# Column sums for the modulation gradients regrouped into runs of 16 and 8 over four strips and two banks, and one w1-gradient piece moved ahead of the last sums

## The chip, the cores and the metric

The kernel runs on one core of a Trainium2 chip. The metric is the device time of one execution in microseconds (us), the median of several runs. Its engines are TensorE (PE, with its weight loads listed apart as PEld), VectorE (DVE), ScalarE (ACT), GpSimdE (POOL) and SyncE (SP). SyncE only issues DMAs here, GpSimdE mostly does.

## The reference

It is the forward and backward pass of one block with adaptive layer norm, in bf16, on 2048 tokens of width 1024 with an MLP of width 3584:

```python
mod = silu(c) @ w_mod                     # six rows of 1024: sa, ca, ga, sb, cb, gb
h = layernorm(x) * (1 + ca) + sa
x = x + ga * irfft2(rfft2(h) * (w_r + 1j * w_i))
h = layernorm(x) * (1 + cb) + sb
out = x + gb * (gelu(layernorm(h) @ w1 + b1) @ w2 + b2)
```

The kernel returns `out` and the gradients by x, w_r, w_i, w1, b1, w2, b2, c and w_mod for a given `grad_out`. The gradient by each of the six modulation rows is a sum over all 2048 tokens, that is, a column sum of a 2048 × 1024 product. These column sums are what the change regroups. From the rows (`d_gmod` in memory) the gradients by w_mod and c follow.

## The kernel before

The work is laid out by the Tile framework. The program calls the operations in some order, a scheduler places them on the engines, and `tc.issue_after` and `behind(ins, later)` tell it that one instruction is to stand after another. Tokens are held as 4 blocks (`b` = 0 to 3, `NB` = 4) of 4 × 128 tokens; `i` is a group of 128 tokens in a block, `h` a half of the 1024 columns (`KH` = 512). The forward pass comes first. Then, in the stretch that matters here:

1. **Backward passes**, `pg_pass(b, h, ...)`: the gradient of a block by the MLP's input, 7 groups `g` × 4 `i` × 4 `k` matmuls `pg<-w1T,gzr` (L1230) into four PSUM banks, for h = 0, then h = 1. "Pass 1, 2, 3" below is b = 1, 2, 3. While PE is in pass b + 1, VectorE and ScalarE work on block b: layer-norm backward (`ln_bwd`, L1370 on VectorE, L1373 on ScalarE, an add at L195) into `gn3` (two buffers in turn, `gn3a`, `gn3b`), the product `pru` = `gn3` · `n2u`, the second layer norm, the residual, the product `au` = gradient · `au` (`au` is loaded from `d_A` at L1521 and multiplied in place), the product with the ga row into `pru`, and the fold of the result for the spectral backward (`fold_quarter`).
2. **Column sums of three rows** for each block: of `gn3`, of `pru`, of `au`. A sum is taken by matmuls against a block of ones, 128 × 32 (`strip_sum`, L217). Their output is only 32 partitions high, a strip; a PSUM bank has four strips (j = 0 to 3). `sums3` (L1398) takes `gn3` into strips 0, 1 of `acc3a` and `pru` into strips 2, 3, one strip for each half h. `sums3_ga` (L1407) takes `au` into all four strips of `acc3b` (`halves_sum`: even and odd `i` apart, added at the end by `store_halves`). The lists `sums_in` hold the matmuls of `sums3` of block b; the next pass puts them behind given matmuls with `behind`: 4 + 4 of `gn3` and 8 of `pru`. The `au` sums come at the end of a pass.
3. **Spectral backward** (`spectral_core`), beside it the products for w2's gradient (`gw2acc`, L1416) and then pieces of w1's gradient (`gw1acc`, L1779; a piece is 16 matmuls and one copy by ScalarE, L1783, and a store by GpSimdE, L1784). `mid_bwd` (L1832) finishes the three rows. `consume_bwd(i, ...)` (L1589) takes the result for block i: layer-norm backward of the first norm, the residual from `d_gx`, the store of x's gradient (two indirect stores, L167), and the column sums `accCA`. `fill(n)` puts n pieces of w1's gradient into PE's stream at that place.
4. **The tail**: the last w1 products by `quad_sums` (sums and differences of operands, seven products for eight; `gqx`, `gqy`, `gqw`, L1695), whose results ScalarE copies (`snap`, L1677) and VectorE combines, and the rest of w_mod's gradient (`otl`, L1299 on ScalarE, stored at L1304 by GpSimdE).

Of the kernel before, what the change touches and what calls it, by code (L numbers as in the profile page):

```python
# [10 lines left out]
FP32 = mybir.dt.float32  # L11
# [8 lines left out]
D = 1024  # L20
# [15 lines left out]
def kernel(  # L36
# [1184 lines left out]
    last_pg = [None]  # L1221
    sums_in = [[], [], []]

    def pg_pass(b, h, pool, before=lambda: ExitStack()):
        pgs = [pool(k)("pg") for k in range(4)]
        for g in range(7):
            for i in range(4):
                for k in range(4):
                    with before():
                        last_pg[0] = nc.tensor.matmul(pgs[i][:], lhsT=gzs[b, g][:, k, i * P:(i + 1) * P],  # L1230
                                                      rhs=w1Ts[g][:, k, h * KH:(h + 1) * KH],
                                                      start=(g == 0 and k == 0), stop=(g == 6 and k == 3))
                    last_pe[0] = last_pg[0]
                g0 = 3 if b == NB - 1 else 2
                if b > 0 and h == 0 and (g, i) in ((g0, 0), (g0 + 1, 2), (g0 + 2, 2)):
                    for ins in sums_in[g - g0]:
                        behind(ins, last_pg[0])
                    sums_in[g - g0].clear()
            for k in range(4 if b < 2 and h == 1 else 0):
# [157 lines left out]

    def sums3(b, g4, p4):  # L1398
        for k, src4 in enumerate((g4, p4)):
            for i in range(4):  # L1400
                for h in range(2):
                    ins = strip_sum(acc3[0], 2 * k + h, src4[:, i, h * KH:(h + 1) * KH], b == 0 and i == 0, b == 3 and i == 3)
                    if b < 3:
                        sums_in[2 * k or i // 2].append(ins)

    def sums3_ga(b, p4):
        halves_sum(acc3[1], p4, b == 0, b == 3)  # L1407

# [48 lines left out]
    for b in range(NB):  # L1457
# [9 lines left out]
        if b > 0:  # L1467
# [10 lines left out]
            for h in range(2):  # L1478
                for _ in pg_pass(b, h, lambda k: ps_f if (8 * (b - 1) + 4 * h + k) % 6 < 4 else ps_s):
                    pass  # L1480
            with tc.issue_after(last_pg[0].ins):
                sums3_ga(b - 1, au)
                if b == NB - 1:
                    gb1_rows()
# [17 lines left out]
        if b < NB - 1:  # L1502
            sums3(b, gn3, pru)
        else:
            g2, ftmp = gn3s[0], gzr[0].rearrange("p a b (c d) -> p (a b c d)", c=1).rearrange("p (q d) -> p q d", d=D)
# [83 lines left out]
    def consume_bwd(i, o4, tmp, tmp2, n1, eb):  # L1589
# [20 lines left out]
        if i < 3:  # L1610
            x1_in = nc.sync.dma_start(out=n1, in_=chunk_rows(d_gx1, i))
        tt(o4, o4, n1 if i < 3 else eb, ALU.add)
        store_tok(out_1, o4, i)
        if i == 1:
            with tc.issue_after(x1_in.ins):
                next(chain)
        fill((4, 1, 2, 2)[i])
        if i == 3:
            for ins in ln_in[-4:]:
                behind(ins, w1g["ev"])  # L1620
        halves_sum(accCA[0], tmp, i == 0, i == 3)
        fill((1, 2, 1, 2)[i])
        if i == 3:
            rows = small.tile([P, D], BF16, tag="gmrow", bufs=1)
            store_halves(accCA[0], rows[0:64, 0:KH], tmp, 1)

# [17 lines left out]
    def quad_sums():  # L1644
# [4 lines left out]
        S3 = reg.tile([P, 8, KH], BF16, name="S3", tag="sma")[:]  # L1649
        tt(T1[:], B12[:], B11[:], ALU.subtract)  # L1650
        tt(T2[:], B22[:], T1[:], ALU.subtract)
# [146 lines left out]
    for cl in (CE, SE):  # L1798
        sm_in = nc.sync.dma_start(out=smA2[:, cl // 2], in_=d_SF[:, cl])
    sums3(3, gn3s[1], pru)  # L1800
    nc.sync.dma_start(out=em2, in_=d_E[:, 0])
# [30 lines left out]
    def mid_bwd():  # L1832
        sums3_ga(3, au)
        rows = small.tile([P, D], BF16, tag="gmrow", bufs=1)
        nc.vector.tensor_copy(out=rows[:, 0:KH], in_=acc3[0][:])
        store_strips(rows[:, 0:KH], 0, 3)
        store_strips(rows[:, 0:KH], 2, 4)
        ins = store_halves(acc3[1], rows[0:64, KH:D], au, 2)
        for step in step_in[3:8]:
            behind(step, ins)  # L1840
# [78 lines left out]
```

## Time and profile before

| | |
|---|---|
| median of 3 runs | 1372.04 us (1367.43 to 1376.55) |
| profiled execution, its own time | 1369.55 us |
| its span | 1367.8 us |
| granted TensorE clock | 0.998 |
| TensorE busy | 1336.9 us, 98% |
| VectorE busy | 1079.9 us, 79% |
| ScalarE busy | 785.1 us, 57% |
| GpSimdE busy | 388.9 us, 28% |

The span goes from the first to the last instruction; some 1.8 us lie around it. All times inside the kernel are counted from the span's start. A timeline row gives the start, the time from the first start to the last end of a group of like instructions, engine, line, operation, output<-inputs, tile, shape and count; in brackets the idle time of the engine before it and what ended that.

### The profile page before, as it was taken

What the parts mean: (1) busy time and instruction counts of PE and PEld (TensorE: products, weight loads), DVE (VectorE), ACT (ScalarE), POOL (GpSimd) and SP (SyncE); (2) the same over time, 40 slices, a digit from 0 to 9 for tenths busy, and PEclk for the clock granted to TensorE, in tenths of its full rate; (3) what the DMA queues carried; (4) which work ended last, traced back from release to release, by engine and by line L of the source; (5) the groups of instructions that cost most, each with busy time, mean ns of one, the idle gap of its engine ahead of it and who ended that gap; (6) DMA issues with size and microseconds to landing.
All of it is one profiled execution on the core that took longest, in us unless ns stands there. A gap on an engine that the chain in (4) does not pass through costs nothing. (4 is left out here: it accounts for less than half of the span.)

```text
span 1367.8 us, 18497 instructions
## 1 busy us (share of the span) xinstructions
PE 1336.9 (98%) x6771; PEld 651.4 (48%) x6899; DVE 1079.9 (79%) x1475; ACT 785.1 (57%) x1112; POOL 388.9 (28%) x436
## 2 busy tenths in 40 slices
PE   6999999999999999999999999999999999999998
PEld 3445566444444444444444444444654555454443
DVE  5997879999988888887611578889888588976996
ACT  4964657667877756665413583446633464544454
POOL 6273542412112122112211011112344330331163
PEclk9999999999999999999999999999999999999999
DMA  9975594899787887697999689998679978899977
GB/s 326 312 209 138 151 267 154 238 280 321 258 256 256 205 265 236 209 280 243 279 290 214 200 206 307 271 285 246 201 220 261 236 158 243 217 235 231 223 259 269
DMA packets 356402, 330.08 MB, mean 241 GB/s; under 512 B 203866, under 2 KB 298736, under 8 KB 356182
## 3 DMA queue, kind: packets, MB, share of 16 engines
q1 hardware_dynamic: 314310, 201.02, 58.1%
q0 software_dynamic: 35232, 120.00, 26.2%
q10 hardware_dynamic: 6768, 7.87, 1.7%
q8 instruction: 54, 0.88, 0.3%
q14 instruction: 38, 0.31, 0.1%
HBM read 165.73 MB, written 114.87 MB: 205 GB/s over the span
## 5 line engine op out<-in xcount | busy, mean ns | idle before, releaser
L1230 PE MATMUL pg<-w1T,gzr 128*128 128x512 bf16 x877 | 194.6, 380 | 1.1 <-issue 0.2
L548 PE MATMUL pp<-gBoT,wt 128*128 128x512 bf16 x810 | 182.8, 379 | 3.6 <-ACT pho L540 1.9
L1076 PEld LDWEIGHTS <-w 128*128 128x128 bf16 x896 | 87.2, 98 | 107.3 <-issue 2.9
L1230 PEld LDWEIGHTS <-gzr 128*128 128x128 bf16 x896 | 86.6, 98 | 108.4 <-issue 5.8
L548 PEld LDWEIGHTS <-wt 128*128 128x128 bf16 x832 | 81.0, 98 | 97.3 <-issue 4.8
L1779 PE MATMUL gw1acc<-gzh,n3n 128*128 128x512 bf16 x500 | 111.1, 380 | 0.6
L1076 PE MATMUL pz<-n3Ta,w 128*128 128x512 bf16 x440 | 98.4, 380 | 1.9 <-ACT gt L1079 1.4
L1076 PE MATMUL pz<-n3Tb,w 128*128 128x512 bf16 x438 | 98.3, 380 | 0.5
L1779 PEld LDWEIGHTS <-n3n 128*128 128x128 bf16 x640 | 62.4, 98 | 75.0 <-issue 1.3
L195 DVE TENSOR_TENSOR ct<-ct 128x2048 bf16<-128x2048 bf16 (+1 forms) x84 | 91.5, 1119 | 4.3 <-ACT n L514 2.0
L1079 ACT ACTIVATE gt<-pz,b_col 128x512 bf16<-128x512 f32 x112 | 72.8, 682 | 37.2 <-PE pz L1076 30.9
L1130 PEld LDWEIGHTS <-hhA 128*128 128x128 bf16 x608 | 58.9, 98 | 73.1 <-issue 2.8
L1087 ACT ACTIVATE gt<-gt 128x2048 bf16<-128x2048 bf16 x28 | 53.5, 1911 | 58.3 <-DVE gt L195 58.3
L1416 PE MATMUL gw2acc<-gB,hhsA 128*128 128x512 bf16 x373 | 84.1, 380 | 0.6
L195 DVE TENSOR_TENSOR gt<-gt,gt 128x2048 bf16<-128x2048 bf16 x56 | 68.4, 1223 | 17.7 <-ACT gt L1089 16.8
L1424 ACT CAST gwo<-gw2acc 128x512 bf16<-128x512 f32 x40 | 23.6, 589 | 87.5 <-PE gw2acc L1416 84.6
L1416 PEld LDWEIGHTS <-hhsA 128*128 128x128 bf16 x384 | 37.6, 98 | 43.4
L1783 ACT CAST gwo<-gw1acc 128x512 bf16<-128x512 f32 x40 | 23.1, 579 | 59.0 <-PE gw1acc L1779 53.8
L1083 ACT ACTIVATE gt<-gt 128x2048 bf16<-128x2048 bf16 x28 | 53.4, 1908 | 3.1 <-DVE hhC L195 2.4
L540 ACT CAST pho<-pp 128x512 bf16<-128x512 f32 x68 | 38.6, 583 | 27.3 <-PE pp L548 24.1
L1089 ACT ACTIVATE gt<-gt 128x2048 bf16<-128x2048 bf16 x28 | 53.4, 1906 | 0.3
L1416 PE MATMUL gw2acc<-gB,otl 128*128 128x512 bf16 x220 | 49.4, 380 | 0.2
(415 smaller groups left out, 2699.7 us busy)
## 6 DMA issues: line engine op xcount, KB each, us to landing
gzr<-d_gz SPq DMA_DIRECT2D x28, 512.0 KB, 4.5
d_ph<-pho POOLq DMA_DIRECT2D x21, 512.0 KB, 6.4
wblk<-in_w_mod_dram SPq DMA_DIRECT2D x10, 1024.0 KB, 7.2
out_dram<-otl POOLq DMA_DIRECT2D x40, 256.0 KB, 4.4
d_hh<-hhA POOLq DMA_DIRECT2D x19, 512.0 KB, 5.9
wrw<-in_w_mod_dram SPq DMA_DIRECT2D x32, 256.0 KB, 5.3
w<-in_B_w_dram SPq DMA_DIRECT2D x7, 1024.0 KB, 11.5
hhC<-d_ph SPq DMA_DIRECT2D x14, 512.0 KB, 3.7
```

The costliest lines, as they stand in the source:

```text
L195: return nc.vector.tensor_tensor(out=out, in0=a, in1=b, op=op)
L540: copy(out=ov, in_=pv)
L548: last_pe[0] = nc.tensor.matmul(pp[:], lhsT=wt[:, fc % 4, cch, :], rhs=gBoT[j][:, cch, :], start=(cch == 0), stop=(cch == NDC - 1))
L1076: last_pe[0] = nc.tensor.matmul(pz[:], lhsT=w1s[g][:, cch, k * P:(k + 1) * P], rhs=n3T[:, cch, :], start=(cch == 0), stop=(cch == NDC - 1))
L1079: z_in = nc.scalar.activation(out=zb[:, k, :], in_=pz[:], func=ACT.Identity, bias=b1_col[:, fc:fc + 1], scale=1.0)
L1083: nc.scalar.activation(out=av, in_=zb, func=ACT.Square)
L1087: nc.scalar.activation(out=sg, in_=bv, func=ACT.Sigmoid, scale=2.0 * GK)
L1089: nc.scalar.activation(out=bv, in_=bv, func=ACT.Sigmoid, scale=-2.0 * GK)
L1130: last_pe[0] = nc.tensor.matmul(pbs[i][:], lhsT=hh[:, k, i * P:(i + 1) * P], rhs=wp[:, k, :], start=False, stop=(g == 6 and k == 3))
L1230: last_pg[0] = nc.tensor.matmul(pgs[i][:], lhsT=gzs[b, g][:, k, i * P:(i + 1) * P], rhs=w1Ts[g][:, k, h * KH:(h + 1) * KH], start=(g == 0 ...
L1416: nc.tensor.matmul(acc[:], lhsT=hh_of(fc)[:, t, :], rhs=gBs[t // 4][:, t % 4, h * KH:(h + 1) * KH], start=(t == 0), stop=(t == NT - 1))
L1779: nc.tensor.matmul(acc[:], lhsT=n3ns[t // 4][:, t % 4, cch * P:(cch + 1) * P], rhs=gz2[t // 8][:, t % 8, :], start=(t == 0), stop=(t == NT ...
```

## The change

It has three parts, and the scheduler rearranges some neighbours with them.

- **Sums.** In each pass there are two places instead of three: `at` is ((3,1), (4,2)) for passes 1 and 2, ((3,2), (5,2)) for pass 3. At the first stand the 8 sums of `gn3`, and in passes 2 and 3 woven with them, two by two, the 8 sums of `au` of the block before, which until now had a run of their own at the end of the pass. `gn3` goes to strips 0, 1 of `acc3a`, `au` to strips 2, 3 of `acc3b`. At the second stand the 8 sums of `pru`, of even `i` into strips 2, 3 of `acc3a`, of odd `i` into strips 0, 1 of `acc3b`. Block 3's sums are written in woven order. The `au` sums at the end of pass 3 stay.
- **Rows.** `mid_bwd` adds the two parts of the `pru` row from two banks and stores the four halves of two rows at the end.
- **w1 piece.** The last sums `accCA` come one piece (16 matmuls) later: `fill` counts 3 and 1 around them instead of 2 and 2. `issue_after` keeps the residual add `w1g["x1"]` ahead of two operations on VectorE and ScalarE.

```diff
-    sums_in = [[], [], []]
+    sums_in = [[], []]
...
-                g0 = 3 if b == NB - 1 else 2
-                if b > 0 and h == 0 and (g, i) in ((g0, 0), (g0 + 1, 2), (g0 + 2, 2)):
-                    for ins in sums_in[g - g0]:
+                at = ((3, 2), (5, 2)) if b == NB - 1 else ((3, 1), (4, 2))
+                if b > 0 and h == 0 and (g, i) in at:
+                    for ins in sums_in[at.index((g, i))]:
                         behind(ins, last_pg[0])
...
-    def sums3(b, g4, p4):
-        for k, src4 in enumerate((g4, p4)):
-            for i in range(4):
-                for h in range(2):
-                    ins = strip_sum(acc3[0], 2 * k + h, src4[:, i, h * KH:(h + 1) * KH], b == 0 and i == 0, b == 3 and i == 3)
-                    if b < 3:
-                        sums_in[2 * k or i // 2].append(ins)
-
-    def sums3_ga(b, p4):
-        halves_sum(acc3[1], p4, b == 0, b == 3)
+    def col_sum(acc, j, src4, i, h, first, last):
+        return strip_sum(acc, j + h, src4[:, i, h * KH:(h + 1) * KH], first, last)
+
+    def sums3(b, g4, p4, a4):
+        for i in range(4):
+            for h in range(2):
+                sums_in[0].append(col_sum(acc3[0], 0, g4, i, h, b == 0 and i == 0, b == 3 and i == 3))
+            for h in range(2 if 0 < b < 3 else 0):
+                sums_in[0].append(sum_ga(b - 1, i, h, a4))
+            for h in range(2 if b == 3 else 0):
+                col_sum(acc3[0], 2, p4, i, h, False, i == 3)
+        for i in range(4 if b < 3 else 0):
+            for h in range(2):
+                sums_in[1].append(col_sum(acc3[i % 2], 2 - 2 * (i % 2), p4, i, h, b == 0 and i < 2, b == 2 and i == 3))
+        if b == 3:
+            sums_in[0].clear()
+
+    def sum_ga(b, i, h, a4):
+        return col_sum(acc3[1], 2, a4, i, h, b == 0 and i == 0, b == 3 and i == 3)
+
+    def sums3_ga(b, a4):
+        for i in range(4):
+            for h in range(2):
+                sum_ga(b, i, h, a4)
...
-            with tc.issue_after(last_pg[0].ins):
-                sums3_ga(b - 1, au)
-                if b == NB - 1:
+            if b == NB - 1:
+                with tc.issue_after(last_pg[0].ins):
+                    sums3_ga(b - 1, au)
                     gb1_rows()
...
-        tt(o4, o4, n1 if i < 3 else eb, ALU.add)
+        w1g["x1"] = tt(o4, o4, n1 if i < 3 else eb, ALU.add)
...
-        fill((4, 1, 2, 2)[i])
+        fill((4, 1, 2, 3)[i])
...
-        fill((1, 2, 1, 2)[i])
+        fill((1, 2, 1, 1)[i])
         if i == 3:
             rows = small.tile([P, D], BF16, tag="gmrow", bufs=1)
-            store_halves(accCA[0], rows[0:64, 0:KH], tmp, 1)
+            with tc.issue_after(w1g["x1"].ins):
+                store_halves(accCA[0], rows[0:64, 0:KH], tmp, 1)
...
-        tt(T1[:], B12[:], B11[:], ALU.subtract)
+        with tc.issue_after(w1g["x1"].ins):
+            tt(T1[:], B12[:], B11[:], ALU.subtract)
...
-        nc.vector.tensor_copy(out=rows[:, 0:KH], in_=acc3[0][:])
+        odd = au[64:128, 0, :].bitcast(FP32)
+        nc.scalar.copy(out=odd, in_=acc3[1][0:64, :])
+        nc.scalar.copy(out=rows[64:128, KH:D], in_=acc3[1][64:128, :])
+        nc.vector.tensor_copy(out=rows[0:64, 0:KH], in_=acc3[0][0:64, :])
         store_strips(rows[:, 0:KH], 0, 3)
+        ins = tt(rows[64:128, 0:KH], acc3[0][64:128, :], odd, ALU.add)
         store_strips(rows[:, 0:KH], 2, 4)
-        ins = store_halves(acc3[1], rows[0:64, KH:D], au, 2)
+        store_strips(rows[:, KH:D], 2, 2)
```

On PE, in pass 2, before: the end of one full matmul group, the four sums of `gn3b` behind group (2,0), and the next group (LDWEIGHTS is the load of a matmul's weights; `ones_bf` are the ones, `gzr` the pass's operand).

```order
L1230 MATMUL pg<-w1T_5957,gzr_5941 128x512
L218 LDWEIGHTS ones_bf
L218 MATMUL acc3a<-gn3b,ones_bf 32x512
L218 LDWEIGHTS ones_bf
L218 MATMUL acc3a<-gn3b,ones_bf 32x512
L218 LDWEIGHTS ones_bf
L218 MATMUL acc3a<-gn3b,ones_bf 32x512
L218 LDWEIGHTS ones_bf
L218 MATMUL acc3a<-gn3b,ones_bf 32x512
L1230 LDWEIGHTS gzr_5941
```

And the start of the first run of pass 2 now, behind group (3,1); it goes on like this to 16.

```order
L1230 MATMUL pg<-w1T_5963,gzr_5941 128x512
L218 LDWEIGHTS ones_bf
L218 MATMUL acc3a<-gn3b,ones_bf 32x512
L218 LDWEIGHTS ones_bf
L218 MATMUL acc3a<-gn3b,ones_bf 32x512
L218 LDWEIGHTS ones_bf
L218 MATMUL acc3b<-au,ones_bf 32x512
L218 LDWEIGHTS ones_bf
L218 MATMUL acc3b<-au,ones_bf 32x512
```

The sums of `gn3b` stand later, all eight together, and between two of them stand two of `au`, on other strips and in the other bank.

On SyncE, whose queue goes in order, the loads around block 1 and pass 3, before (`hb` are transposes of the MLP's activations, `gzr` the operand of the passes, `n3u`, `n2u`, `got` rows of the next block):

```order
L1206 DMA gzr2_5943<-d_gz_104 128x4x512
L1521 DMA au_6287<-d_A_98 128x4x1024
L1453 DMA_TRANSPOSE hb_6760<-d_hh_103 128x16x128
L1453 DMA_TRANSPOSE hb_6763<-d_hh_103 128x16x128
L1206 DMA gzr2_5943<-d_gz_104 128x4x512
L1461 DMA n3u_6280<-d_n3_99 128x4x1024
L1463 DMA n2u_6281<-d_x1_97 128x4x1024
L1206 DMA gzr3_5944<-d_gz_104 128x4x512 x2
```

And now:

```order
L1206 DMA gzr2_5943<-d_gz_104 128x4x512
L1467 DMA_TRANSPOSE hb_6760<-d_hh_103 128x16x128
L1467 DMA_TRANSPOSE hb_6763<-d_hh_103 128x16x128
L1206 DMA gzr2_5943<-d_gz_104 128x4x512
L1475 DMA n3u_6280<-d_n3_99 128x4x1024
L1535 DMA au_6287<-d_A_98 128x4x1024
L1477 DMA n2u_6281<-d_x1_97 128x4x1024
L1206 DMA gzr3_5944<-d_gz_104 128x4x512 x2
```

The load of `au` has moved behind two transposes and two loads, since its buffer is read by the sums until later.

On GpSimdE in the tail, before: the stores of w1 pieces, the last two indirect stores of x's gradient, and the stores of w_mod rows.

```order
L1784 DMA out_dram<-gwo_9683 128x512 x11
L167 DMA out_dram<-ct,xu 2048x1024 x2
L1784 DMA out_dram<-gwo_9683 128x512 x2
L1304 DMA out_dram<-otl 128x1024
L1784 DMA out_dram<-gwo_9683 128x512
```

And now:

```order
L1800 DMA out_dram<-gwo_9684 128x512 x12
L167 DMA out_dram<-ct,xu 2048x1024 x2
L1800 DMA out_dram<-gwo_9684 128x512
L1304 DMA out_dram<-otl 128x1024
L1800 DMA out_dram<-gwo_9684 128x512
```

One store of a w1 piece has come ahead of the indirect stores.

More of the change, by code (lines that the diff above doesn't have):

```diff
@@ L1233, in pg_pass @@
                     last_pe[0] = last_pg[0]
[L1234 to L1236 removed]
+                at = ((3, 2), (5, 2)) if b == NB - 1 else ((3, 1), (4, 2))
+                if b > 0 and h == 0 and (g, i) in at:
+                    for ins in sums_in[at.index((g, i))]:
                         behind(ins, last_pg[0])
[L1238 removed]
+                    sums_in[at.index((g, i))].clear()
             for k in range(4 if b < 2 and h == 1 else 0):
@@ L1502 @@
         if b < NB - 1:
-            sums3(b, gn3, pru)
+            sums3(b, gn3, pru, au)
         else:
@@ L1799 @@
         sm_in = nc.sync.dma_start(out=smA2[:, cl // 2], in_=d_SF[:, cl])
-    sums3(3, gn3s[1], pru)
+    sums3(3, gn3s[1], pru, au)
     nc.sync.dma_start(out=em2, in_=d_E[:, 0])
```

## The prediction

> **What bounds the kernel now.** I read the page's first part, then the list of TensorE's waits, then the timelines of the two places that the diff touches. The first part says which engine to follow:
>
> ```profile
> span 1367.8 us, 18497 instructions
> PE 1336.9 (98%) x6771; PEld 651.4 (48%) x6899; DVE 1079.9 (79%) x1475; ACT 785.1 (57%) x1112; POOL 388.9 (28%) x436
> ```
>
> TensorE (PE) is busy in 1336.9 of 1367.8 us. Only what takes time from its stream, or lets it wait, can move the end. The list of PE's waits (engine, line, what it waited for; us in total, times, longest) has these at or behind the places of the change:
>
> ```profile
> PE accCA L218 <- DVE ct L195: 1.3, 1, 1.3
> ...
> PE gqy L1695 <- ACT snap L1677: 0.9, 1, 0.9
> ...
> PE gw2acc L1416 <- issue: 0.3, 2, 0.2
> ```
>
> The first stands ahead of the last column sums, which the moved w1 piece concerns. The second comes 40 us later, in the tail. The third is the largest of PE's waits between 880 and 1275 us, so a lead that PE wins in the backward passes should last until 1275.
>
> A "busy" PE is not at full pace in the column sums. This is PE's timeline (start, us from first start to last end, line, tile, count) of pass 1, of an `au` run with the start of pass 3, and of block 3's run of 16:
>
> ```profile
> 774.49 5.35 PE L1230 MATMUL pg<-w1T,gzr 128*128 128x512 bf16 x23
> 779.77 0.61 PE L218 MATMUL acc3a<-gn3a,ones_bf 128*32 128x512 bf16 x4
> 780.32 3.63 PE L1230 MATMUL pg<-w1T,gzr 128*128 128x512 bf16 x16
> 783.87 1.04 PE L218 MATMUL acc3a<-pru,ones_bf 128*32 128x512 bf16 x8
> 784.85 1.47 PE L1230 MATMUL pg<-w1T,gzr 128*128 128x512 bf16 x6
> ...
> 868.26 0.61 PE L218 MATMUL acc3b<-au,ones_bf 128*32 128x512 bf16 x8
> 868.80 11.40 PE L1230 MATMUL pg<-w1T,gzr 128*128 128x512 bf16 x51
> 880.13 0.61 PE L218 MATMUL acc3a<-gn3a,ones_bf 128*32 128x512 bf16 x4
> 880.67 5.35 PE L1230 MATMUL pg<-w1T,gzr 128*128 128x512 bf16 x23
> ...
> 939.22 1.89 PE L1416 MATMUL gw2acc<-gB,hht 128*128 128x512 bf16 x8
> 941.04 0.39 PE L218 MATMUL acc3a<-gn3b,ones_bf 128*32 128x512 bf16 x2
> 941.07 0.39 PE L218 MATMUL acc3a<-pru,ones_bf 128*32 128x512 bf16 x2
> ...
> 941.73 0.38 PE L218 MATMUL acc3a<-pru,ones_bf 128*32 128x512 bf16 x2
> 942.04 1.69 PE L1416 MATMUL gw2acc<-gB,hht 128*128 128x512 bf16 x6
> ```
>
> The reader is to see what a switch between full matmuls and strip sums costs. By the code 52 full matmuls lie between 868.80 and 880.13 and 24 between 774.49 and 779.77 (a record is missing in each row). With pitch p and entry e (last full matmul to first sum), 51p + e = 11.33 and 23p + e = 5.28, so p = 0.216 us and e = 0.31 us. From the first sum to the next full matmul a run takes the difference of two starts. What a run adds to the stream is e, plus that difference, less the p that the step would take anyway:
> - 4 matmuls on two strips: 780.32 − 779.77 = 0.55, adds 0.64
> - 8 on two strips: 0.98, adds 1.07
> - 8 on four strips (`au`): 0.54, adds 0.64
> - 16 on four strips: 1.00, adds 1.09
>
> Each round of one matmul for every strip takes about p, whether two strips take part or four. A run also pays about 0.2 us for being a run at all. Fewer runs and fuller rounds are the whole mechanism.
>
> **The sums, step by step.** Pass 1 loses 4 + 4 + 8 (two strips), 0.64 + 0.64 + 1.07 = 2.35, and gets one 8 on two strips and one 8 on four, 1.07 + 0.64 = 1.71: **−0.64**. Passes 2 and 3 lose the same 2.35 and get a 16 and an 8 on four strips, 1.09 + 0.64 = 1.73: **−0.62 each**. The two `au` runs at the ends of passes 1 and 2 disappear: **−0.64 each**. Block 3's 16 were already executed two strips and two strips in turn, so their new program order is worth nothing. Together −3.16 us.
>
> One price isn't in the trace: a run whose four strips lie in two banks (`acc3a` and `acc3b`). At best it is the run of 16 above. At worst the banks exclude each other and the rounds go at the pace of two strips: a 16 adds 1.09 + 4 × 0.216 = 1.95, an 8 adds 1.07; pass 1 then saves 2.35 − 2.14 = 0.21, passes 2 and 3 lose 0.67 each, the `au` runs still save 1.28, and of 3.16 there remain 0.15. I take the first, since the row nearest in every other respect (16 matmuls, four strips, two sources) shows it.
>
> From 941.07 to 941.73 three rounds of the run of 16 took 0.66 us, 0.22 each. The Trainium skill speaks against such a pace in "TensorE: Matmul & The Clock Gate", section "Part 3: Packing small matmuls — row/col tiling": it lists a measured speedup of 2.38× with three column tiles, 0.79 for each tile. An estimate from that page: four tiles would give 3.2×, a round 0.27 us, and with ten more rounds on four strips than before (14 less the `au` runs' 4) the sums would save 0.5 us less, 2.6 instead of 3.16. The trace disagrees with its 0.22.
>
> **Earlier sums meet later data.** A run may start when its source is there. VectorE (DVE) and the SyncE queue (SPq), around pass 3; the last two rows are DMA groups of the page (KB each, median us to landing):
>
> ```profile
> 830.55 0.44 SPq L1521 DMA_DIRECT2D au<-d_A  x1
> ...
> 843.20 0.46 SPq L1461 DMA_DIRECT2D n3u<-d_n  x1
> 843.71 0.50 SPq L1463 DMA_DIRECT2D n2u<-d_x  x1
> ...
> 848.59 2.29 DVE L195 TENSOR_TENSOR au<-gn3b,au 128x4096 bf16<-128x4096 bf16 x1
> ...
> 855.90 2.36 DVE L195 TENSOR_TENSOR gn3b<-pru 128x2048 bf16<-128x2048 bf16 x2 [2.83 <-DMA d_gx<-gn3b]
> ...
> 878.96 0.69 DVE L195 TENSOR_TENSOR gn3a<-gn3a,got 128x1024 bf16<-128x1024 bf16 x1
> ...
> 880.41 0.69 DVE L195 TENSOR_TENSOR gn3a<-gn3a,got 128x1024 bf16<-128x1024 bf16 x1 [0.77 <-ACT got L1373]
> ...
> wblk<-in_w_mod_dram SPq DMA_DIRECT2D x10, 1024.0 KB, 7.2
> ...
> w<-in_B_w_dram SPq DMA_DIRECT2D x7, 1024.0 KB, 11.5
> ```
>
> In pass 3 the run of 16 stands behind group (3,2), eight full matmuls behind the old place (3,0). In old time that is 880.67 + 8 × 0.216 = 882.40 for the next start. Off come the run at (3,0), 0.64, and the lead from before, 0.64 + 0.64 + 0.62 + 0.64 = 2.54: 879.22. The first sum would start 0.09 later (e less p), and the fourth round, which takes `gn3a`'s last quarter, at 879.31 + 3 × 0.22 = 879.97. That quarter is ready at 880.41 + 0.69 = 881.10, and this chain is DVE's and ScalarE's (ACT), not PE's. So PE waits about **+1.1 us** with the whole pass behind it. The third quarter (879.65) is just in time.
>
> The second bound on that wait is the `au` load. It was issued at 830.55, before the `hb` transposes; now it stands between the loads of `n3u` and `n2u`, since its buffer is free only after the sums in pass 2. If it is issued near 843.7 and lands as the faster of the two groups of 1024 KB does (7.2), it is there at 850.9, 2.3 us after DVE wanted it at 848.59. Behind that multiply DVE has 2.83 us idle at 855.90, which hides the 2.3. Earlier transposes (1024 KB less ahead of them) make it less. I take 0; the slower group (11.5) would make it 855.2 − 848.59 − 2.83, +3.8, the far end.
>
> **The moved piece, and the end.** PE (with VectorE, ScalarE, GpSimdE, which is POOL) around the last sums and the tail:
>
> ```profile
> 1273.75 3.83 PE L1779 MATMUL gw1acc<-gzh,n3n 128*128 128x512 bf16 x17
> ...
> 1276.56 2.29 DVE L195 TENSOR_TENSOR ct<-ct,xt 128x4096 bf16<-128x4096 bf16 x1
> ...
> 1278.90 0.61 PE L218 MATMUL accCA<-ct,ones_bf 128*32 128x512 bf16 x8 [1.32 <-DVE ct L195]
> ...
> 1299.03 2.29 DVE L195 TENSOR_TENSOR ct<-ct,eb 128x4096 bf16<-128x4096 bf16 x1
> ...
> 1301.61 3.41 POOL L167 DMA_INDIRECT out_dram<-ct,xu  x1 [10.58 <-DVE ct L195]
> ...
> 1309.00 1.31 POOL L1784 DMA_DIRECT2D out_dram<-gwo  x2
> 1310.30 0.54 POOL L1304 DMA_DIRECT2D out_dram<-otl  x1
> ...
> 1312.96 1.15 ACT L1299 ACTIVATE otl<-gr,u_rt 128x1024 bf16<-128x1024 bf16 x1 [4.66 <-DMA out_dram<-otl]
> ...
> 1318.31 0.56 ACT L1677 COPY snap<-gqy 128x512 f32<-128x512 f32 x1
> ...
> 1318.92 1.89 PE L1695 MATMUL gqy<-gzh,ct 128*128 128x512 bf16 x8 [0.88 <-ACT snap L1677]
> ```
>
> Sixteen more full matmuls (16 × 0.216 = 3.46 us) go ahead of the sums and cover the 1.32 us there: −1.32 at that place. But the wait at 1318.92 doesn't hang on PE. The chain is the DVE product (1276.56), the rest of that chain on DVE up to 1299.03, two indirect stores on POOL, the queue of POOL stores, ACT's wait for `otl` to leave, `snap`. A PE that comes 1.32 earlier waits 1.32 longer: +1.32. Of the order on POOL one L1784 store less stands between the indirect stores and the first L1304 (0.65 of the 1.31), so `snap` comes some 0.65 earlier: **−0.65**, the net of the move.
>
> The lead from the passes comes through if the chain shifts with PE. It does where the stage's transposes wait for PE to free their buffers. This row of SyncE's waits, from 1180 to 1290 us, says so:
>
> ```profile
> SPq L1634 <- PE gw1acc L1779: 56.9, 7, 16.1
> ```
>
> What is reordered on DVE, ACT and SyncE between the passes and the spectral stage I cost at nothing: an ACT copy more for the third row (0.56 by the copy at 1318.31), and two more row stores on SyncE ahead of the `hhsA` transpose:
>
> ```profile
> 980.92 0.53 SPq L229 DMA_DIRECT2D d_gmod<-rows  x2
> ```
>
> They lie beside PE's spectral matmuls, where no wait of PE is listed. With that cover gone they would cost 0.56 and 0.53.
>
> **Sum.** −3.16 + 1.1 − 0.65 = −2.7 us on the profiled execution's 1369.55 us. That execution lies 2.5 under the median of the runs (1372.04; they spread over 9 us), and I apply the same difference to the median: **1369.3 us**. Within 1% (13.7 us) is about what a measurement of this kernel can tell from no change.
>
> **Rivals.**
> - *Everything counts* (0.10): `gn3a` is ready in time because DVE's chain comes earlier too, and `snap` follows the product. −3.16 − 1.32 = −4.5: 1367.5. Against it: DVE at 855.90 waited for a store, not for PE.
> - *The tail keeps its own time* (0.20): between 1190 and 1280 the DMA, not PE, sets the product's time, so `snap` stays and every lead ends in the wait before it. Only the 0.65 is left: 1371.4. The row of 56.9 us speaks against it, the 1.32 of waiting for DVE for it.
> - *Two banks exclude each other* (0.07): 0.15 from the sums, no wait in pass 3, 0.65 at the end: 1371.2.
> - *Slower* (0.13): the `au` load. It sits in SyncE's queue ahead of `n2u`, and behind it on DVE stand the multiply, the product with the ga row and the whole fold before `gn3a`. Landing 2.83 us late (851.4) costs nothing; from there each us is one of PE's in pass 3, and beyond 2.83 + 2.7 (landing after 854.1) the change loses. A load as slow as the other group's (11.5) lands at 855.2: 1.1 over the median, 1373.1.
> - That the change doesn't do what it says I exclude for the sums: the order of instructions shows the runs, and only their pace is open.
>
> **How the numbers follow.** The forecast has 0.45; the remaining 0.05 are shifts of DMA traffic without a name, of either sign. All cases lie between 1367.5 and 1373.1. The median of a few runs whose spread is 9 us adds about 2 on either side: **1365.5 to 1375.5**. Nothing with a price reaches 13.7 us: faster by over 1% 0.02, within 1% 0.95, slower by over 1% 0.03.
>
> **What would show it.** Right: seven runs of sums in the three passes and at their ends instead of twelve; runs of 16 of 1.0 us on two banks; a PE wait of about 1 us for `gn3a` in pass 3; no wait at the last sums, and one of some 1.5 to 2 us before 1318. Wrong: rounds of 0.43 us; a DVE wait for `au`; no shift of the product at 1276; or a wait of PE at the spectral stage, where none is now.

## The result, and the profile after

The changed kernel takes 1382.08 us (median of 6 runs, 1378.78 to 1384.44) against 1370.04 us for the kernel before (6 runs, 1366.53 to 1376.55) beside it. The ratio of the runs is 1.0084, with a 95% interval of 1.0061 to 1.0107; here and below it is not the quotient of the two medians. The forecast was 1369.3 us, between 1365.5 and 1375.5: the sign and the range were both wrong, and only the bound of 1% held. The profiled execution took 1381.39 us, 11.84 more than the one of before (1369.55). First the page of the changed kernel:

```profile
span 1379.6 us, 18500 instructions
PE 1340.1 (97%) x6771; PEld 652.3 (47%) x6899; DVE 1082.1 (78%) x1476; ACT 784.9 (57%) x1112; POOL 398.1 (29%) x436
```

TensorE has as many recorded instructions as before and is busy 3.2 us longer, though the sums were to get cheaper. The other 8.6 us of the span are idle time of PE. Its list of waits (what PE was about to do, what it waited for; us in total, times, longest) names two that before had hardly or not at all:

```profile
PE gqy L1711 <- ACT snap L1693: 6.0, 1, 6.0
...
PE pg L1230 <- ACT gn3a L1246: 3.8, 1, 3.8
```

The first was 0.9 before. The second is new. PE's timeline around them (start, us from first start to last end, count; in brackets the idle time ahead and what ended it) shows the sums, too:

```profile
829.98 0.39 PE L218 MATMUL acc3a<-gn3b,ones_bf 128*32 128x512 bf16 x2
829.99 0.39 PE L218 MATMUL acc3b<-au,ones_bf 128*32 128x512 bf16 x2
...
830.65 0.38 PE L218 MATMUL acc3b<-au,ones_bf 128*32 128x512 bf16 x2
831.19 4.26 PE L1230 MATMUL pg<-w1T,gzr 128*128 128x512 bf16 x19 [0.16 <-issue]
...
873.61 14.07 PE L1230 MATMUL pg<-w1T,gzr 128*128 128x512 bf16 x51 [3.83 <-ACT gn3a L1246]
887.61 0.39 PE L218 MATMUL acc3a<-gn3a,ones_bf 128*32 128x512 bf16 x2
...
982.40 1.04 PE L218 MATMUL acc3b<-au,ones_bf 128*32 128x512 bf16 x8
...
1275.77 11.17 PE L1795 MATMUL gw1acc<-gzh,n3n 128*128 128x512 bf16 x50
1286.87 0.62 PE L218 MATMUL accCA<-ct,ones_bf 128*32 128x512 bf16 x8
...
1328.57 3.57 PE L1711 MATMUL gqy<-gzh,ct 128*128 128x512 bf16 x8 [6.01 <-ACT snap L1693]
```

The reader is to see four things. The run of 16 on two banks keeps the pace: from 829.98 to its fourth round at 830.65 (the `au` half) 0.67 us, 0.22 a round. The wait ahead of `accCA` is gone. Eight `au` sums at 982.40 now take 1.04 us instead of 0.62 (on two strips, as the sums of `au` now always are). And behind the two large waits the matmuls are slow: eight `gqy` in 3.57 us, where before 8 took 1.89, and 51 `pg` in 14.07 us, where before 51 took 11.40. The view by windows (stretch, us, PE busy with its count, then PEld, DVE, ACT, POOL; the granted clock; DMA share; GB/s) says how slow:

```profile
830.00:865.00 35.00, 34.68 (x176) 15.52 (x180) 27.85 (x31) 9.91 (x15) 6.02 (x7) 1.00 0.98 312
...
869.00:874.00 5.00, 1.17 (x6) 0.37 (x5) 4.07 (x5) 4.94 (x7) 0.00 (x0) 0.82 1.19 159
874.00:879.00 5.00, 5.00 (x13) 1.81 (x12) 3.82 (x8) 2.62 (x7) 1.14 (x2) 0.50 0.98 210
879.00:884.00 5.00, 4.95 (x23) 2.25 (x23) 4.37 (x7) 3.42 (x4) 0.00 (x0) 0.99 1.04 393
```

Between 874 and 879 the granted clock was 0.50: 13 matmuls, where the next 5 us hold 23. "Half pace" below means this. The first row, used below, is the stretch ahead, in which the loads for pass 3 compete: the DMA engines are busy all the time (0.98), VectorE and ScalarE aren't.

The same matmul can be looked up in both timelines. The difference of its two starts, from place to place, is the whole account of the 11.84 us:

| from, to | what happens there | us |
|---|---|---|
| start to pass 1 | nothing changed there; the executions differ | +1.11 |
| passes 1 and 2, their `au` runs | fewer runs, less 0.5 of pauses (0.36 for a load of `gzr`, 0.16) | −2.04 |
| start of pass 3 | wait 3.83 and its surroundings, 3.94 | +3.94 |
| behind it | about 13 matmuls at half pace | +2.74 |
| pass 3 | fewer runs | −0.64 |
| `au` of blocks 2 and 3 | 8 on two strips instead of four, twice | +0.80 |
| last sums | piece ahead of them, no wait | −1.39 |
| `snap` | wait 6.01 instead of 0.88 | +5.13 |
| behind it | about 10 matmuls at half pace | +2.19 |

The sums and the piece saved 3.3 us net, and two waits with their half pace cost 14.0.

**Where the wait of pass 3 comes from.** SyncE's issues, VectorE and ScalarE of the changed kernel:

```profile
844.11 0.46 SPq L1535 DMA_DIRECT2D au<-d_A  x1
844.62 1.00 SPq L1477 DMA_DIRECT2D n2u<-d_x  x1
...
855.38 2.29 DVE L195 TENSOR_TENSOR au<-gn3b,au 128x4096 bf16<-128x4096 bf16 x1 [5.76 <-DMA au<-d_A]
...
859.90 2.36 DVE L195 TENSOR_TENSOR gn3b<-pru 128x2048 bf16<-128x2048 bf16 x2
...
862.61 4.64 ACT L514 ACTIVATE n2u<-n2u,stats 128x1024 bf16<-128x1024 bf16 x4 [15.71 <-DMA n2u<-d_x]
868.46 1.15 ACT L1264 ACTIVATE gn3b<-fbuf,al 128x1024 bf16<-128x1024 bf16 x1 [1.21 <-DVE pru L195]
872.80 0.67 ACT L1246 ACTIVATE gn3a<-pg,stats 128x512 bf16<-128x512 f32 x1
```

And the same three places on ScalarE before:

```profile
853.97 4.64 ACT L514 ACTIVATE n2u<-n2u,stats 128x1024 bf16<-128x1024 bf16 x4 [8.01 <-DMA n2u<-d_x]
...
864.47 1.15 ACT L1264 ACTIVATE gn3b<-fbuf,al 128x1024 bf16<-128x1024 bf16 x1 [5.85 <-DVE pru L195]
...
868.80 0.67 ACT L1246 ACTIVATE gn3a<-pg,stats 128x512 bf16<-128x512 f32 x1
```

The `au` load was used 11.3 us after its issue. VectorE waited 5.76 us for it and began the multiply at 855.38 instead of 848.59, 6.8 us late. Two operations on, before the change, VectorE had waited 2.83 us for a store (the row at 855.90 in the prediction). That operation now starts at 859.90 without a wait. So 2.83 us of the delay are hidden, and 4.0 us go on through VectorE's chain to `pru`. ScalarE's fold (L1264), which waits for `pru`, came 4.0 us later, and behind it L1246, the copy that empties a PSUM bank of pass 2. Pass 3 needs that bank for its third group. PE came 0.9 us earlier than before, and before there had been 1.06 us of room (worked out below under `repaired_nopiece`): 4.0 + 0.9 − 1.06 makes the 3.83 within 0.1.

The load of `n2u`, issued right behind `au`, was late too: it was used at 862.61 instead of 853.97. Its normalization (L514) stands ahead of the fold on ScalarE, whose idle time of 15.71 us looks like the cause. It isn't, in this execution: L514 was done at 867.25, and ScalarE then waited another 1.21 us for VectorE's `pru`. The fold starts when the later of two routes is there, VectorE's from `au` or ScalarE's from `n2u`. Here it was VectorE's.

**Where the wait for `snap` comes from.** GpSimdE, VectorE and ScalarE in the changed kernel's tail:

```profile
1306.28 4.61 POOL L167 DMA_INDIRECT out_dram<-ct,xu  x1 [10.58 <-DVE ct L195]
1311.20 9.36 POOL L167 DMA_INDIRECT out_dram<-ct,xu  x1 [0.30 <-issue]
...
1306.52 1.27 DVE L195 TENSOR_TENSOR sr<-sr 1x512 f32<-1x512 f32 x2
...
1309.92 1.28 DVE L195 TENSOR_TENSOR sr<-sr 1x512 f32<-1x512 f32 x2
1311.12 2.27 DVE L195 TENSOR_TENSOR gzh<-gzh,gzh 128x4096 bf16<-128x4096 bf16 x1
1313.33 0.74 DVE L200 CAST row<-sr 1x512 bf16<-1x512 f32 x2
...
1322.42 2.29 DVE L195 TENSOR_TENSOR ct<-gzu,gzh 128x4096 bf16<-128x4096 bf16 x1 [2.74 <-issue]
...
1323.86 1.15 ACT L1299 ACTIVATE otl<-gr,u_rt 128x1024 bf16<-128x1024 bf16 x1 [11.03 <-DMA out_dram<-otl]
...
1327.94 0.58 ACT L1693 COPY snap<-gqy 128x512 f32<-128x512 f32 x1
```

And before:

```profile
1305.32 3.68 POOL L167 DMA_INDIRECT out_dram<-ct,xu  x1 [0.30 <-issue]
...
1305.24 2.27 DVE L195 TENSOR_TENSOR gzh<-gzh,gzh 128x4096 bf16<-128x4096 bf16 x1
1307.44 1.27 DVE L195 TENSOR_TENSOR sr<-sr 1x512 f32<-1x512 f32 x2
```

The second of the two indirect stores took 9.36 us instead of 3.68. `otl` is stored behind it on GpSimdE, ScalarE waited 11.03 us for that (4.66 before), and `snap` stands behind that wait. On VectorE the order had changed: of four small fp32 additions on `sr` (1 × 512), a pair stood behind each of two `gzh` subtractions; now each pair stands ahead of its subtraction, and two small copies of the result (`row<-sr`) follow the second subtraction at once. This probably comes from the `issue_after` on the first subtraction, which was not tried by itself.

### The profile page after: what moved, and what is told of

It reads as the page before. It is cut to its first block, busy times and chain, and to the rows that moved or that the text cites. A ratio compares the mean times of both kernels' runs of the same rounds, so it can differ in the third digit from the quotient of the medians.

```text
span 1379.6 us, 18500 instructions
## 1 busy us (share of the span) xinstructions
PE 1340.1 (97%) x6771; PEld 652.3 (47%) x6899; DVE 1082.1 (78%) x1476; ACT 784.9 (57%) x1112; POOL 398.1 (29%) x436
## 5 line engine op out<-in xcount | busy, mean ns | idle before, releaser
L1230 PEld LDWEIGHTS <-gzr 128*128 128x128 bf16 x896 | 87.6, 99 | 114.1 <-issue 11.3
L195 DVE TENSOR_TENSOR gt<-gt,gt 128x2048 bf16<-128x2048 bf16 x56 | 68.4, 1223 | 17.7 <-ACT gt L1089 16.8
```

The lines of the kernel that those rows point to most:

```text
L195: return nc.vector.tensor_tensor(out=out, in0=a, in1=b, op=op)
```

## The experiments

All ratios are against the kernel before on the same chip, with 95% intervals. Theory: the move of the `au` load and the order on VectorE in the tail cost the time, each by itself. Rivals: the regrouped sums or the moved piece cost it.

**au_early.** The `au` load of blocks 1 and 2 goes to GpSimdE's queue, away from `n2u`.

```diff
-        nc.sync.dma_start(out=au[:], in_=chunk_rows(d_A, b))
+        (nc.gpsimd if b in (1, 2) else nc.sync).dma_start(out=au[:], in_=chunk_rows(d_A, b))
```

> The changed kernel with the loads of au for blocks 1 and 2 issued by GpSimdE (ahead of its d_gx store) instead of SyncE; nothing else moves on any engine. Theory (late au load): DVE's wait for au before block 1's multiply (5.76 us) goes, PE's wait for the evacuation of the banks at the start of pass 3 (3.83 us) goes with the 12 or 13 matmuls at half pace behind it (2.5 us), and a wait of about 1 us for gn3a's last quarter may appear: 5.4 to 6.5 us less, 1375.6 to 1376.7 against 1382.1. The wait for snap in the tail stays at 5 to 6 us. Rival (sums over two banks or their new places make PE wait): no change, 1382. Rival (the tail keeps its own time): the wait goes, but the wait for snap grows by as much, 1382.

Measured: 1376.54 us, 1.0053 (1.0034 to 1.0073). The median lies in the expected range, but by luck: the wait that was to go is still there. VectorE no longer waited for `au`, yet PE's wait for the bank was 6.9 us in the profile, which fell on the slowest of the nine runs (1385.26). SyncE issued `n2u` 5.8 us later than in the changed kernel (850.42), and it landed later still:

```profile
866.34 4.63 ACT L514 ACTIVATE n2u<-n2u,stats 128x1024 bf16<-128x1024 bf16 x4 [20.82 <-DMA n2u<-d_x]
```

Here the fold follows L514 without a wait, so ScalarE's route set it. A VectorE free of the wait isn't enough: both loads must land in time. What the other queue does for `n2u` isn't clear: in `both`, with the same queues, `n2u` was issued at 844.55 and used at 857.79.

**tail_order.** The changed kernel with the old order of VectorE in the tail.

```diff
+        t1 = tt(T1[:], B12[:], B11[:], ALU.subtract)
+        t2 = tt(T2[:], B22[:], T1[:], ALU.subtract)
+        for k, ins in enumerate(w1g["sr"]):     # the four additions of sr
+            behind(ins, t1 if k < 2 else t2)
```

> The changed kernel with the four fp32 sr additions on DVE back behind the two gzh subtractions, as in the kernel before; the moved w1 piece, the order on PE, ACT, POOL and SyncE stay. Theory (DVE's order starves the second indirect store): that store takes 3 to 4 us instead of 9.36, the wait for snap falls from 6.0 to 1 to 1.5 us and the half pace behind it (2.2 us) goes: 6.5 to 7.3 us less, 1375 to 1375.6. The au wait and PE's 3.83 us in pass 3 stay. Rival (the moved w1 piece and the GpSimdE order it brings make the store late): no change, 1382.

Measured: 1377.27 us, 1.0057 (1.0034 to 1.0079). This is more than the expected 1375 to 1375.6. The stores are back at 3.41 and 3.68 us, and no wait for `snap` is listed. PE's wait at pass 3 was 11.1 us in this execution, and a PE that comes so late leaves `snap` more time; so the durations of the stores are the evidence here.

```profile
1309.62 3.41 POOL L167 DMA_INDIRECT out_dram<-ct,xu  x1 [9.68 <-DVE ct L195]
1313.34 3.68 POOL L167 DMA_INDIRECT out_dram<-ct,xu  x1 [0.30 <-issue]
```

**both.** The two edits together.

> Both repairs on the changed kernel. Theory: both add up, 12 to 13.5 us less than 1382.1: 1368.6 to 1370, that is the kernel before (1370.0) within 1.5 us. What the sums save (2.3 by the trace, 3.16 less twice 0.43 for au runs on two strips) is then eaten in part by the wait for gn3a in pass 3 (1 us). Rival (a third cause): over 1373.

Measured: 1373.09 us, 1.0024 (1.0007 to 1.0041), with PE's wait at pass 3 down to 1.72 in the second fastest of the twelve runs. This is lower than either alone, though the intervals overlap a little, and it misses the expected 1368.6 to 1370: the kernel before isn't reached.

**before_tail.** The reverse: the kernel before, with nothing but the new order of VectorE in the tail.

```diff
+        with tc.issue_after(w1g["sr"][1].ins):
             tt(T1[:], B12[:], B11[:], ALU.subtract)
+        with tc.issue_after(w1g["sr"][3].ins):
             t2 = tt(T2[:], B22[:], T1[:], ALU.subtract)
```

> The kernel before with DVE's order in the tail as in the changed kernel: the four sr additions and the row casts ahead of the gzh subtractions; PE, ACT, POOL and SyncE keep their order, no w1 piece moves. Theory (DVE's order): the second indirect store grows from 3.68 to 8 to 9 us, PE's wait for snap from 0.88 to over 5 us with about 2 us at half pace behind it if it passes some 3.5 us: 1375 to 1377.5 against 1370.0. Rival (the moved piece): no change, 1370.

Measured: 1372.9 us, 1.0038 (1.0024 to 1.0051). The order alone makes the store slow, without any of the sums. GpSimdE and PE:

```profile
1300.17 9.37 POOL L167 DMA_INDIRECT out_dram<-ct,xu  x1 [0.30 <-issue]
...
1318.01 3.46 PE L1699 MATMUL gqy<-gzh,ct 128*128 128x512 bf16 x8 [2.44 <-ACT snap L1681]
```

The wait for `snap` was 2.44 us (expected: over 5). It was enough for half pace: the next group starts at 1321.31, so the eight matmuls took 3.30 us from start to start, 0.41 each.

**repaired.** The changed kernel with the old order in the tail, and with block 1's `au` load ahead of the two transposes again, that is, four transfers earlier in SyncE's queue. It was issued at 830.64, as before the change.

```diff
+        with tc.issue_after(au_lds[1].ins) if len(au_lds) == 2 else ExitStack():
             turns.append(nc.sync.dma_start_transpose(out=hb[:], in_=src))
```

> The changed kernel with the tail order of DVE repaired as in the run tail_order, and block 1's au load back on SyncE ahead of the two hb transposes where the kernel before had it; PE, ACT and POOL keep the changed order. Theory (the stretch from 830 to 865 us is bound by DMA, and what lands late there is whatever stands last: au in the changed kernel, n2u in au_early): au lands before 845 and n2u near 854 as in the kernel before, L514 doesn't stand in ACT's way, PE's wait at the start of pass 3 goes below 1 us in the profile and the executions lose their slow half. Ratio 0.997 to 1.001 (2.3 us from the sums, less about 1 us for gn3a's last quarter). Rival (the new places of the sums, not the load, cost): the ratio stays at 1.002 or above as in the run both.

Measured: 1369.13 us, 1.0006 (0.9994 to 1.0017): no different from before. It differs from `tail_order` (1.0034 to 1.0079) in the place of the load and in one load of `gzr`, which changed places with `n3u`. The intervals are apart: the place of the load costs about 0.5% in the changed kernel. But the profile still has `n2u` late, and a wait of PE (expected: below 1 us):

```profile
862.23 4.64 ACT L514 ACTIVATE n2u<-n2u,stats 128x1024 bf16<-128x1024 bf16 x4 [17.50 <-DMA n2u<-d_x]
...
871.74 12.50 PE L1233 MATMUL pg<-w1T,gzr 128*128 128x512 bf16 x44 [4.13 <-ACT gn3a L1249]
```

This execution took 1371.12 us, above its median. The fold follows L514 without a wait, so here `n2u` set it. How late the loads land differs from execution to execution, but the place of `au` shows through: with it right ahead on SyncE `n2u` was used 17.0 to 21.2 us after its own issue (`kept_warm`, the changed kernel, `fp32_gap`, `tail_order`, `before_aulate`), without it 10.3 to 16.8 (the kernel before, `before_tail`, `both`, `repaired_nopiece`, `au_early`, `repaired`). The two ranges only just miss each other.

**before_aulate.** The kernel before, with block 1's `au` load moved between `n3u` and `n2u`.

```diff
         n3_ld = nc.sync.dma_start(out=n3u[:], in_=chunk_rows(d_n3, b))
+        if b == 2:
+            behind(au_lds[1], n3_ld)
```

> The kernel before with only block 1's au load moved, to the place between the n3u and n2u loads on SyncE that the changed kernel gives it. All else, the sums too, stays. Theory (late load): DVE waits 3 to 7 us for au, n2u lands 5 to 9 us later, and PE waits 3 us or more for the evacuation of the banks at the start of pass 3, with a stretch at half pace if the wait passes some 3.5 us: ratio 1.003 to 1.006. Rival (the load is harmless by itself; the sums' places do it): ratio 1.000, no wait of PE at pass 3.

Measured: 1371.18 us, 1.0026 (1.0004 to 1.0048). Its runs lie between 1366.58 and 1382.95, and the profile caught the worst. VectorE:

```profile
865.16 2.29 DVE L195 TENSOR_TENSOR au<-gn3b,au 128x4096 bf16<-128x4096 bf16 x1 [16.78 <-DMA au<-d_A]
```

PE then waited 12.7 us for the bank. `n2u` was late too, but the fold waited another 4.20 us for VectorE's `pru`. The move of one load, alone, is slower by a little on the whole (just under the expected 1.003 to 1.006), and the slowest execution is 14.7 us over the median of the kernel before.

**fp32_gap.** The changed kernel with two more additions of 1 × 512 fp32 numbers, whose result nobody reads, behind the second `gzh` subtraction.

```diff
+            for _ in range(2):
+                t2 = tt(spent[:, 0:KH], spent[:, 0:KH], spent[:, KH:D], ALU.add)
```

> The changed kernel with two superfluous fp32 additions on DVE (1 partition, 512 elements, 0.6 us each) behind the second gzh subtraction and the row casts, on spent data. Theory (GpSimdE writes an indirect store's descriptors only while DVE isn't in one of the long bf16 operations): the second indirect store ends within these 1.2 us, 3.5 to 5 us instead of 9.36, and the wait for snap falls from 6.0 to 1.5 to 3 us without half pace behind it: 5 us less, 1377. Rival (its length is set by the DMA queue or by the data): it stays at 9.4 us, and snap comes 1.2 us later.

Measured: 1373.84 us, 1.0038 (1.0016 to 1.0061), and no wait for `snap`. GpSimdE and VectorE:

```profile
1301.07 4.61 POOL L167 DMA_INDIRECT out_dram<-ct,xu  x1 [7.51 <-DVE ct L195]
1305.98 3.08 POOL L167 DMA_INDIRECT out_dram<-ct,xu  x1 [0.30 <-issue]
...
1304.71 1.27 DVE L195 TENSOR_TENSOR sr<-sr 1x512 f32<-1x512 f32 x2
1305.91 2.27 DVE L195 TENSOR_TENSOR gzh<-gzh,gzh 128x4096 bf16<-128x4096 bf16 x1
1308.11 0.74 DVE L200 CAST row<-sr 1x512 bf16<-1x512 f32 x2
1308.79 1.39 DVE L195 TENSOR_TENSOR sr<-sr 1x512 f32<-1x512 f32 x2
```

Superfluous work on VectorE made the store three times as fast. The ends of the stores say when one gets through. Here they are 1305.68 and 1309.06: 0.97 us after VectorE began the `sr` additions at 1304.71, and 0.95 after it began the small copies at 1308.11. In the changed kernel the first ends at 1310.89, 0.97 after the additions at 1309.92. The second doesn't end in the 0.74 us of the small copies at 1313.33, but at 1320.56, where VectorE has a pause (the 2.74 us ahead of 1322.42). What follows the pause, `ct<-gzu,gzh`, writes the part of `ct` that this store reads: by the code, VectorE stops there because it needs the store done. So in these four places a store ends 0.9 to 1.0 us after VectorE begins a stretch without a bf16 operation on 128 partitions. That isn't the whole rule. The additions at 1306.52, 0.24 us into the first store, didn't let it through. And in the old order the second store ends 1.56 us after its additions began (1309.00 and 1307.44 in the kernel before). The other four profiles with the new order (`au_early`, `kept_warm`, `before_tail` and the changed kernel) all have 4.61 and 9.36 or 9.37, the nine with the old order all 3.41 and 3.68 or 3.69.

The Trainium skill has a rule that bears on this in "SBUF — State Buffer", section "Who interferes with whom": a VectorE instruction with two inputs in SBUF contends with a GpSimdE instruction that reads SBUF. The 9.36 us beside the `gzh` subtractions agree with it. The `sr` additions don't: they have two such inputs as well and let the store end (0.97 us). What GpSimdE reads while it works on a store, no run here shows.

**kept_warm.** The changed kernel, with the first two groups of pass 3 computed three times (16 superfluous matmuls, 3.46 us), so that PE works while the bank is late.

```diff
-            for i in range(4):
+            for j, i in enumerate((0, 1) * 3 + (2, 3) if (b, h, g) == (3, 0, 0) else range(4)):
```

> The changed kernel with sixteen superfluous matmuls at the start of pass 3: the groups (0,0) and (0,1) are computed three times over, which leaves the result as it is. They run while PE would wait for the banks of groups (0,2) and (0,3). Theory (a wait of some 3.5 us or more halves TensorE's pace for 5 us): the wait in pass 3 shrinks by 3.45 us to 0.5 to 3 us, the 12 or 13 matmuls behind it take 216 instead of 427 ns, 2.5 us less: 1379.5, ratio to the kernel before 1.0065 against 1.0084. Rival (the half pace has another cause, such as the load of DMA): it stays, and the time is that of the changed kernel or up to 1 us more.

Measured: 1381.28 us, 1.0102 (1.0074 to 1.013), not better than the changed kernel and far from the expected 1.0065. The profile fell on the fastest run (1371.42 us). There 0.25 us of the wait are left, and the next window has the full clock:

```profile
872.00:877.00 5.00, 4.80 (x22) 2.25 (x23) 4.35 (x8) 2.62 (x9) 1.15 (x2) 1.00 0.92 170
```

Without the idle time, the half pace didn't come. On the time it is inconclusive: where the bank isn't late the extra work would cost its 3.46 us, and there is no profile of a slower run.

**repaired_nopiece.** `repaired` without the moved w1 piece.

```diff
-        fill((4, 1, 2, 3)[i])
+        fill((4, 1, 2, 2)[i])
...
-        fill((1, 2, 1, 1)[i])
+        fill((1, 2, 1, 2)[i])
```

> The run repaired with the w1 piece back behind the last sums (fill 2 and 2). Theory (the wait at the last sums is swallowed by the wait for snap, and only one store's place on GpSimdE, 0.65 us, is left): 0 to 0.7 us slower than repaired, ratio 1.0006 to 1.0011. Rival (the piece's full 1.3 us counts): 1.0016. Rival (the piece costs): below 1.0003.

Measured: 1369.13 us, 1.0014 (1.0005 to 1.0022), against 1.0006 (0.9994 to 1.0017) with the piece. The piece didn't make the loss, and its worth (1.1 us by the two ratios) isn't resolved. The profile of this run shows where the lead of the passes goes even when no load holds up the fold. PE, and ScalarE ahead of it:

```profile
870.62 11.38 PE L1233 MATMUL pg<-w1T,gzr 128*128 128x512 bf16 x51 [1.97 <-ACT gn3a L1249]
...
865.47 1.15 ACT L1267 ACTIVATE gn3b<-fbuf,al 128x1024 bf16<-128x1024 bf16 x1 [1.27 <-DVE pru L195]
```

By the same account as above PE is 2.05 us ahead of before at the end of pass 2, and nothing of it is left after this wait (870.62 against 870.53). Before, the copy of 868.80 ended 869.47, and PE needed the bank at 868.80 + 8 × 0.216 = 870.53: there was 1.06 us of room. A lead of 2.05, and a fold 1.0 us later than before's 864.47, use it up and make the wait. The fold waited for VectorE's `pru` here, and VectorE had waited 3.96 us for a store of `d_gx`, not for a load.

**repaired_n2, before_n2, late_n2.** The normalization of `n2u` (L514) is put behind other work of ScalarE, so that a late `n2u` no longer stops the fold: in `repaired`, in the kernel before, and in `tail_order`.

```diff
+        if b == 2:
+            for ins in n2_norm:
+                behind(ins, ln_act[0])
```

> The run repaired, with ACT's four L514 (the normalization of n2u for block 2) moved behind the last of its four L1373 on n3u, so that neither the fold (L1263, L1264) nor the evacuation of the banks (L1246) stands behind the landing of n2u. Theory (what is left in repaired is n2u landing late at the head of ACT's queue): PE's wait at the start of pass 3 (4.1 us in repaired) goes below 2 us, the sums' 2.3 us show, and the executions draw together: ratio 0.997 to 0.9995 against 1.0006. Rival (DVE's own waits for d_gx set the fold): the wait and the ratio stay. Price: pru of block 2 comes about 3 us later, harmless if PE's sums of it at (5,2) don't wait.

> The kernel before with the same move of the four L514, as the control for repaired_n2. Theory: the kernel before has n2u in time in its profile (5.85 us of slack at L1264), and only its slower executions gain: ratio 0.998 to 1.000. The difference to repaired_n2 is then what the sums and the moved piece are worth by themselves, 1 to 2.3 us. Rival (pru 3 us later makes PE wait): 1.001 or more.

> The run tail_order (au late) with the same move of the four L514. It parts the two ways of the late load: au on DVE and n2u on ACT. Theory (both count, n2u more in the slow executions): ratio 1.002 to 1.004 against 1.0057 of tail_order; DVE's wait for au stays. If n2u were all of it: 1.000 or below. If au on DVE were all of it: 1.005 or above.

Measured: 1372.43 us, 1.0035 (1.0022 to 1.0048); 1372.63 us, 1.0034 (1.0022 to 1.0046); 1374.58 us, 1.0061 (1.0039 to 1.0084). All miss: the move costs about 0.3% where nothing was broken. In `repaired_n2` the wait for `gn3a` did fall, from 4.13 to 1.99 us, but the other buffer became late. PE there:

```profile
899.16 6.20 PE L1233 MATMUL pg<-w1T,gzr 128*128 128x512 bf16 x21 [3.21 <-ACT gn3b L1249]
```

In `late_n2`, where `n2u` stops nothing, VectorE:

```profile
856.83 2.29 DVE L195 TENSOR_TENSOR au<-gn3b,au 128x4096 bf16<-128x4096 bf16 x1 [8.67 <-DMA au<-d_A]
```

PE still waited 7.2 us for the bank: a late `au` is enough by itself, as the changed kernel's own trace says. No version beat the kernel before.

## Why the prediction was wrong

- **The `au` load: "I take 0" was the step that failed.** The place, the queue and VectorE's chain up to the fold were described (the rival *Slower*, 0.13), and the end that I gave up, +3.8 with a landing after 11.5 us, was what the execution showed: 11.3 us, of which 4.0 came through, and a wait of 3.83. I had taken the faster of two groups of the page, measured in other stages, for a queue that had just been given one more load. Where PE would meet it was wrong, too: the sum has PE's wait at the sums of `gn3a` within pass 3, and it came at the start of the pass, at the bank that ScalarE empties behind the fold. That 3.8 and 3.83 agree so well is luck: the lead of 0.9 and the room of 1.06 nearly cancel. That `n2u` behind `au` becomes late as well wasn't priced; in the changed kernel's trace it had 1.21 us to spare, in `au_early` and `repaired` it set the fold.
- **The order on VectorE in the tail had no term.** I costed the reordering "at nothing" for the stretch up to the spectral stage, and in the tail compared the new order only on PE and GpSimdE. The two indirect stores went into the chain with before's durations, as if they were fixed. They depend on VectorE's neighbours: 3.68 or 9.36 us. `before_tail` shows it alone, 0.38% (0.24 to 0.51).
- **Idle time counted once, where it costs more.** A wait of 3.83 us cost 6.7, one of 6.01 cost 8.2, through matmuls at half pace. The sum had no such term; 4.9 of the 11.84 us are this.
- **The sums: right in mechanism and pace, with one term missed.** Two banks run at 0.22 a round, so that rival is out. Pass 1 saved 0.64 as forecast, and so did pass 3 (0.62). But the `au` sums of blocks 2 and 3 went onto two strips, and 0.64 became about 1.05 each (+0.80): of 3.16 us 2.36 are left by this term. I had read that they "stay" where they are, not on which strips.
- **The wait of 1.1 us for `gn3a`'s last quarter** didn't appear at that place in the repaired kernels. PE waits at the start of pass 3 instead, for the bank (1.97 in `repaired_nopiece`). The idea that a lead meets a chain that doesn't depend on PE was right; which chain was wrong, and it takes nearly the whole lead.
- **The moved piece** did what was said at the last sums: −1.39, and no wait there. That `snap`'s chain swallows it isn't shown: in the changed kernel the slow store made that wait, and in `repaired` and `repaired_nopiece` neither a wait for `snap` nor one at the last sums is listed. The −0.65 from one store less can't be told from zero.

What is open: what else decides when `au` and `n2u` land (with `au` right ahead the landings of `n2u` still lie 4.2 us apart, without it 6.5), what lets an indirect store through beyond the 0.9 us, why `kept_warm` has the median it has, and what the piece is worth.

## What to carry to other kernels

When a regrouping makes a buffer live longer, price the load that refills it by the slowest landing that the trace shows, follow who stands behind it in the same queue, and behind those on their engines. Where two late routes meet, ask which came last: it is named where the meeting operation waits, and the longest idle time need not be it (here 15.71 us on ScalarE did no harm, 1.21 us told the cause). Compare the order on every engine around a critical chain, not only the one whose work is changed: four small additions moved on VectorE cost about as much here as the late load. A saving on PE is worth no more than the room at the next place where PE meets a chain of its own clock; look for that room (here 1.06 us) before adding up what is saved.

## What the runs showed of the hardware

- After a pause of PE the matmuls run at about 0.42 instead of 0.216 us for a while (eight `gqy` from 1328.57 to the next start at 1331.94). On top of the wait this cost 2.7 us after one of 3.83, 2.2 after 6.01 and 1.6 after 2.44. After the single waits of 1.72 and 1.97 us in `both` and `repaired_nopiece` it didn't come; in `before_n2`, after two waits of 1.03 and 1.17 us with 1.0 us of work between them, it did (granted clock 0.57 from 902 to 904). The Trainium skill, "TensorE: Matmul & The Clock Gate", section "Part 1: The HAM clock gate", has the half rate after one idle window of about 3.4 us, with windows that run freely. The clock of 0.50 agrees; that 2.44 us was enough doesn't follow from a whole idle window.
- An indirect store on GpSimdE took 3.08 us where VectorE had a stretch without large bf16 operations at the right place, 9.36 us where it had none. It ended 0.9 to 1.6 us after such a stretch began.
- In the stretch from 830 to 865, where the DMA engines are busy throughout (0.98), a load of 1024 KB that was waited for was used 10.1 to 21.2 us after its issue; `n2u` took 17.0 to 21.2 us with one more load right ahead of it in the queue, 10.3 to 16.8 without. The medians of the page's groups, 7.2 and 11.5 us, say little about such a stretch.
